# Chunk 0 of a fused Mamba-2 scan and gated feed-forward layer: two units of 64 tokens of four sequences, and one VectorE operation to join converted weights

## The chip, the core and the metric

The kernel runs on one core of a Trainium2 chip. A core has five engines with a queue each, which run side by side and wait for one another by semaphores: TensorE (PE; its weight loads are listed as PEld), VectorE (DVE), ScalarE (ACT), GpSimd (POOL) and SyncE (SP), which here only issues transfers. PE writes to PSUM, a memory of eight banks; POOL cannot read PSUM. The metric is the device time of one execution in microseconds, as the median of several runs.

## What is computed

The inputs are x (4 sequences, 8 heads, 768 tokens, 32 channels), a (4, 8, 768), B and C (4, 8, 768, 16), all float32, and two weight matrices `w_in` (256 x 2048) and `w_out` (2048 x 256), which arrive as float64. The output has 3072 rows of 256. Cut to its core:

```python
cum = np.cumsum(np.log(np.clip(a, 1e-06, 1.0)), axis=-1)       # in a chunk of tokens
L = causal * np.exp(cum[..., :, None] - cum[..., None, :])
y = ((C @ B.T) * L) @ x + (C @ state) * np.exp(cum)[..., None]
state = np.exp(cum_end) * state + (B * np.exp(cum_end - cum)).T @ x
...
h = y.reshape(B*S, H*D) @ w_in
out = (h * np.cos(h)) @ w_out
```

The result of the scan does not depend on how long the chunks are.

## The kernel before

**Chunks and steps.** The scan is done in six chunks of 128 tokens of all four sequences. Each chunk gives `yT`, 512 rows of the feed-forward layer. The layer goes through them in 16 steps a chunk: step n does `first(n)`, four matmuls of 256 columns each (L578) that give `hp` from 256 rows and 256 of the 2048 middle columns, then the gate (`k` on ACT L582, `w` on DVE L584, the cosine on ACT L589, the product `gT` on DVE L594), and, two steps later (`LAG`), `second(n)`, four matmuls (L637) that add the step's share to the output. In chunk 0, `turn_of` has step n do the rows of sequence pair u = n % 2 and middle columns of piece j = n // 2. From chunk 1 on `second` goes another way, with seven products instead of eight and sums formed on POOL (`differ`, `differ_w`).

**The weights.** They are float64 words and are converted in the kernel, in eight pieces for each matrix (256 middle columns a piece). `fetch` loads a piece. `grade` has ACT take the magnitude of the upper word (L222, `mag`) and the lower word's top bits (L220, `last`), and POOL clamp `mag` (L223). `join` has DVE shift and mask `mag` (L236), put the sign in (L238), and POOL add the two parts as integers into `w_in` or `w_out` (L246). In the loop over steps, step n grades the piece of step n+1 and joins its own: `out_j` at step 2j, `in_j` at step 2j-3. Piece `in_j` is first read by `first(2j)`, piece `out_j` by `second(2j)`.

**Chunk 0.** Sequence by sequence: `a` is spread over the partitions by matmuls against a one-hot matrix (`spread_a` L332), a scan on DVE gives the decays inside each half of 64 tokens (`decays0` L342), a matmul the decays across the halves (`cross`), PE transposes B and C (`turn`), multiplies them (`intra` L407), DVE applies the decays (L414), and PE multiplies by x (`finish` L424). Three of the four sequences are finished ahead of step 0, the fourth and the states handed to chunk 1 (`sum_up` L537, `carry` L547) in steps 0 to 2. `fill` (L101) puts matmuls without use on PE.

**Order.** The schedule is written out by hand: the order of the program is the order in every engine's queue. All loads are issued from SP, in program order: `a`, then B, C and x of three sequences, piece `in_0`, the fourth sequence, then the pieces, then the loads of chunk 1 (`rest_of_loads`). Chunks 1 and on read `a` clipped and in two forms that the kernel writes to memory itself (`a_cut`, `a_all`, L757) before it loads them again.

Of the kernel before, what the change touches and what calls it, by code (L numbers as in the profile page):

```python
# [16 lines left out]
LEAST = 2.0 ** -15  # L17
# [8 lines left out]
def kernel(  # L26
# [10 lines left out]

# [54 lines left out]
    def load(c, seqs=(0, NB), only=(B, C, x)):  # L108
# [8 lines left out]
        for dst, src in ((bc[:, 0], B), (bc[:, 1], C), (xr, x))[::2 if c > 1 else 1]:  # L117
# [3 lines left out]
            halves = c > 0 and src is not C  # L121
# [9 lines left out]

    def by_blocks(c, u):
        return c > 1

    def load_blocks(c, u):


# [33 lines left out]
    a0 = const.tile([P, P], FP32, name="a0")  # L171
    a0z = const.tile([P, P], FP32, name="a0z")
    nc.sync.dma_start(out=a0[0:NB * H], in_=a[:, :, 0:P].rearrange("b h p -> (b h) p"))
    for r in (slice(NB * H, W), slice(W, P)):
        V.memset(a0[r], 1.0)
# [31 lines left out]
    def grade(which, i, later=False, n=1):  # L207

# [6 lines left out]
        held[which, i] = list(zip(high, shares(which, mag.bitcast(U32), n), lasts))  # L217
# [3 lines left out]
        for e in range(n):  # L221
            ACT.activation(mags[e], high[e].bitcast(FP32), AF.Abs)  # L222
            G.tensor_scalar(out=mags[e], in0=mags[e], scalar1=MOST, scalar2=LEAST,  # L223
                            op0=ALU.min, op1=ALU.max)
            if not later:
                rest(e)
# [3 lines left out]
    def join(which, i):  # L230

        parts = held.pop((which, i), ())
        for e, (high, bits, last) in enumerate(parts):
            V.tensor_scalar(out=bits, in0=bits, scalar1=3, scalar2=0x3FFFFFFF,  # L236
                            op0=ALU.logical_shift_left, op1=ALU.bitwise_and)
            V.scalar_tensor_tensor(out=bits, in0=high, scalar=0xC0000000, in1=bits,  # L238
                                   op0=ALU.bitwise_and, op1=ALU.bitwise_or)
            dst = kept(which, i)  # L240
            if len(parts) > 1:
                dst = dst[:, :, e * P:(e + 1) * P]
            else:
                bits, last = (ap.rearrange("p (k f) -> p k f", k=dst.shape[1])
                              for ap in (bits, last))
            G.tensor_tensor(out=dst.bitcast(U32), in0=bits, in1=last, op=ALU.add)  # L246

    for b in range(NB):
        if b == NB - 1:
            fetch("in", 0)  # L250
        load(0, (b, b + 1))
    nc.sync.dma_start(
        out=a_in, in_=a.rearrange("(u b) h (c p) -> (b h c) u p", u=NU, p=P))
    for w in (("in", 1), ("out", 0), ("in", 2), ("out", 1), ("in", 3)):
        fetch(*w)
# [5 lines left out]
    V.memset(quarter, HALF_PI)  # L261


    unit = const.tile([P, HH * P + W], FP32, name="unit")
    G.tensor_copy(out=unit[:, 0:HH * P].rearrange("p (h i) -> p h i", h=HH),
                  in_=ident.unsqueeze(1).to_broadcast([P, HH, P]))


    ms = [scan.tile([P, 2 * H * W], FP32, tag=f"m{b}", bufs=1, name="m") for b in range(NB)]
    m_of = [t.rearrange("p (e h i) -> p e h i", e=2, h=H) for t in ms]  # L270
    m_at = [t.rearrange("p (h i) -> p h i", h=H) for t in ms]
    unit0, tos = m_of[NB - 1][:, 0], m_of[NB - 1][:, 1]
    for t in range(2):
        ts = slice(t * W, (t + 1) * W)
        V.tensor_copy(out=unit0[ts], in_=ident[ts, ts].unsqueeze(1).to_broadcast([W, H, W]))

    slot = const.tile([P, 2], FP32, name="slot")
# [7 lines left out]

    ACT.activation(const.tile([P, 1], FP32, name="sine"), quarter, AF.Sin)


    clip = dict(scalar1=1.0, scalar2=1e-6, op0=ALU.min, op1=ALU.max)
    G.tensor_scalar(out=a0z, in0=a0, **clip)  # L290
    G.memset(a0z[:, 0:P:W], 0.0)
    V.tensor_scalar(out=a0, in0=a0, **clip)


    to = const.tile([P, W], FP32, name="to")
    V.tensor_tensor_scan(out=to, data0=a0[:, W:P], data1=ones[:, 0:W], initial=1.0,
                         op0=ALU.mult, op1=ALU.mult)
    fro = const.tile([P, W], FP32, name="fro")
    V.memset(fro, 1.0)
    V.tensor_tensor_scan(out=fro[:, W - 2::-1], data0=a0[:, W - 1:0:-1],  # L300
                         data1=ones[:, 0:W - 1], initial=1.0, op0=ALU.mult, op1=ALU.mult)
    fros = const.tile([P, NB, W], FP32, name="fros")
    V.tensor_tensor(out=fros, in0=fro.unsqueeze(1).to_broadcast([P, NB, W]),
                    in1=those.unsqueeze(2).to_broadcast([P, NB, W]), op=ALU.mult)
    V.tensor_reduce(out=slot, in_=ident.rearrange("p (k t n) -> p t k n", t=2, n=N),
                    axis=mybir.AxisListType.XY, op=ALU.add)


    a0s = m_of[NB - 2]
    halves = a0z.rearrange("p (t i) -> p t i", t=2)  # L310
    for h in range(HH):
        ACT.activation(a0s[:, :, h], halves, AF.Copy, scale=mine[:, h:h + 1])
    for t in range(2):
        G.tensor_tensor(out=a0s[:, t, HH:H], in0=halves[:, t:t + 1].to_broadcast([P, HH, W]),
                        in1=mine[:, HH:H].unsqueeze(2).to_broadcast([P, HH, W]), op=ALU.mult)
    G.tensor_tensor(out=tos, in0=to.unsqueeze(1).to_broadcast([P, H, W]),
                    in1=mine.unsqueeze(2).to_broadcast([P, H, W]), op=ALU.mult)


# [4 lines left out]

    spread = {}

    def spread_a(b, tag):


        spread[b] = ps = bank([P, H, W], "a_ps", tag)  # L330
        for t in range(2):
            PE.matmul(ps[t * W:(t + 1) * W], lhsT=those[:, b:b + 1].to_broadcast([P, W]),  # L332
                      rhs=a0s[:, t], start=True, stop=True, tile_position=(0, t * W),
                      skip_group_check=True)

    def decays0(b):

        lam[0, b] = l = scan.tile([P, 2, H, W], FP32, tag="lam", bufs=4, name="lam")  # L340
        flat = "p h i -> p (h i)"
        V.tensor_tensor_scan(out=l[:, 0].rearrange(flat), data0=spread.pop(b).rearrange(flat),  # L342
                             data1=unit0.rearrange(flat), initial=0.0,
                             op0=ALU.mult, op1=ALU.add)
        G.tensor_copy(out=l[W:P, 1], in_=l[W:P, 0])
        G.memset(l[W:P, 0], 0.0)

    def cross(b, tag):

        ps = bank([P, H, W], "l_ps", tag)  # L350
        PE.matmul(ps, lhsT=fros[:, b:b + 2].rearrange("p b j -> p (b j)"), rhs=tos,
                  start=True, stop=True)
        for t in range(2):
            ACT.copy(out=lam[0, b + t][0:W, 1], in_=ps[t * W:(t + 1) * W])
            weigh(0, b + t)

    def weigh(c, b):

        scaled[c, b] = sc = scan.tile([P, H, N], FP32, tag="sc", bufs=NB, name="sc")
        l = lam[c, b][:, :, P - 1:P] if c > 0 else lam[c, b][:, 1, :, W - 1:W]  # L360
        G.tensor_tensor(out=sc, in0=raw[c][0][:, 0, heads(b)],
                        in1=l.to_broadcast([P, H, N]), op=ALU.mult)
# [23 lines left out]

    def turn(b, tag=None):

        bc = raw[0][0]
        tp = (pair("tp")[:, 0] if tag is None else bank([P, 4 * P], "tp", tag)  # L390
              ).rearrange("p (k i) -> p k i", k=4)
        for k in range(2):
            PE.transpose(tp[:, k], bc[:, k, heads(b)].rearrange("p h n -> p (h n)"), ident)

        cT = scan.tile([P, 2, P], FP32, tag="cT", name="cT")
# [340 lines left out]
    for b in range(NB):  # L736
        decays0(b)
# [177 lines left out]
```

## Time and profile before

| | |
|---|---|
| median of 3 runs | 376.96 us (376.90 to 377.03) |
| span of the profiled execution | 374.9 us |
| PE busy | 367.1 us (98%) |
| DVE busy | 286.0 us (76%) |
| POOL busy | 215.1 us (57%) |
| ACT busy | 176.0 us (47%) |
| `first(0)` starts | 17.81 us |
| `second(0)` starts | 25.71 us |
| clamp of a piece on POOL, L223, 128x512 | 0.61 to 0.93 us |
| shift and mask on DVE, L236, 128x512, mean from 25 to 72 us | 0.47 us |
| sign on DVE, L238, 128x512, mean from 25 to 72 us | 0.85 us |
| add on POOL, L246, 128x512 | 1.27 us |

The profiled execution is one run; its span goes from the first to the last instruction, and the device time of a run has about 2 us of launch and end around it. The busy share of PE is taken from modelled ends of matmuls and is no measure of how well it is used. In lines of the chain of waits the first column is the start in us, the second the time taken, then the engine and the line. In lines of the timeline the idle time before an instruction and what ended it stand in brackets. In lines of the waits the three numbers are the total in us, the count and the longest.

### The profile page before, as it was taken

The numbers are of one execution on the slowest core, as the hardware profiler recorded it, in microseconds if no ns is written. First come the engines' busy times: TensorE is split into PE (matmuls) and PEld (weight loads), VectorE is DVE, ScalarE is ACT, GpSimd is POOL, SyncE is SP. The second block draws the span as 40 slices with busy tenths as digits, with TensorE's granted clock in tenths as the row PEclk, the third lists the DMA queues.
The fourth block names the chain that finished last, engine by engine and source line by source line (L and its number), as shares of the span: only waits on it lengthen the run. The fifth ranks groups of instructions, "written<-read, shape, count | busy, mean of one in ns | idle before, by whom it ended". The sixth has DMA issues, their size and how long they took to land.

```text
span 374.9 us, 8382 instructions
## 1 busy us (share of the span) xinstructions
PE 367.1 (98%) x3108; PEld 325.4 (87%) x3108; DVE 286.0 (76%) x478; ACT 176.0 (47%) x304; POOL 215.1 (57%) x335
## 2 busy tenths in 40 slices
PE   8999999999999999999999999999999999999996
PEld 3478888889899899999899998999999989999995
DVE  8879999889799957987767987766887872554543
ACT  3887666544344434344334445434444443443442
POOL 6767555589946346665354693353775344444451
PEclk9999999999999999999999999999999999999999
DMA  7989896514545741663322655121020000010011
GB/s 84 263 239 285 243 219 117 128 15 99 151 92 78 131 108 16 84 153 77 76 54 21 91 141 131 25 51 17 4 41 8 11 21 2 0 30 0 2 28 29
DMA packets 124424, 31.52 MB, mean 84 GB/s; under 512 B 93568, under 2 KB 120288, under 8 KB 124384
## 3 DMA queue, kind: packets, MB, share of 16 engines
q1 hardware_dynamic: 124224, 30.86, 38.4%
q8 instruction: 24, 0.39, 0.4%
q14 instruction: 16, 0.13, 0.1%
q10 hardware_dynamic: 160, 0.13, 0.1%
HBM read 27.64 MB, written 3.34 MB: 83 GB/s over the span
## 4 chain that ended last, share of the span: by engine, by line
PE 83%; SPq 5%; POOL 4%; DMA 3%; DVE 2%; issue 1%; ACT 1%; POOLq 0%; DVEq 0%; ACTq 0%
PE hp L578 40%; PE o L675 29%; PE o L637 7%; SPq L127 4%; PE y L516 3%; PE g L474 2%; DMA words<-in_moe_w_in_dram 1%; POOL words L613 1%; PE y L509 1%; POOL gd L619 1%; DMA bc<-in_B_dram 1%; DMA blocks<-in_C_dram 1%; POOL gd L622 1%; PE o L720 1%; PE s_ps L537 0%
## 5 line engine op out<-in xcount | busy, mean ns | idle before, releaser
L578 PE MATMUL hp<-yT,w_in 128*128 128x256 f32 x768 | 183.7, 382 | 1.9 <-DVE gT L594 1.4
L578 PEld LDWEIGHTS hp<-yT,w_in 128*128 128x128 f32 x768 | 139.4, 190 | 21.6 <-issue 2.0
L619 POOL TENSOR_TENSOR gd<-gT 128x256 f32<-128x256 f32 x79 | 59.2, 750 | 100.0 <-DVE gT L594 91.2
L589 ACT ACTIVATE w<-w,quarter 128x512 f32<-128x512 f32 x96 | 69.2, 721 | 76.8 <-DVE w L584 76.7
L582 ACT ACTIVATE k<-hp 128x512 int32<-128x512 f32 x96 | 57.2, 595 | 82.3 <-PE hp L578 82.0
L584 DVE SCALAR_TENSOR_TENSOR w<-hp,k 128x512 f32<-128x512 f32 x96 | 65.4, 681 | 37.3 <-ACT k L582 37.1
L594 DVE TENSOR_TENSOR gT<-hp,w 128x512 f32<-128x512 f32 x96 | 65.2, 679 | 34.6 <-ACT w L589 24.8
L675 PE MATMUL o<-words,gd 128*128 128x128 f32 x474 | 65.9, 275 | 0.0
L675 PEld LDWEIGHTS o<-words,gd 128*128 128x128 f32 x474 | 59.3, 192 | 0.1
L378 DVE TENSOR_TENSOR_SCAN lam<-arow,unit 128x512 f32<-128x512 f32 x40 | 57.0, 1426 | 0.0
L675 PEld LDWEIGHTS o<-w_out,gT 128*128 128x128 f32 x316 | 47.5, 191 | 4.0
L622 POOL TENSOR_TENSOR gd<-gT,gd 128x128 f32<-128x128 f32 x79 | 45.5, 577 | 6.2
L675 PE MATMUL o<-w_out,gT 128*128 128x128 f32 x316 | 48.0, 274 | 0.0
L621 POOL TENSOR_TENSOR gd<-gT,gd 128x128 f32<-128x128 f32 x79 | 44.2, 560 | 6.2
L495 DVE TENSOR_TENSOR m<-g,lam 128x256 f32<-128x256 f32 x80 | 30.9, 415 | 0.5
L637 PE MATMUL o<-w_out,gT 128*128 128x256 f32 x128 | 30.3, 380 | 0.4 <-POOL w_out L246 0.4
L675 PE MATMUL o<-w_out,gd 128*128 128x128 f32 x158 | 30.6, 275 | 0.0
L675 PE MATMUL o<-words,gT 128*128 128x128 f32 x158 | 30.6, 275 | 0.0
L637 PEld LDWEIGHTS o<-w_out,gT 128*128 128x128 f32 x128 | 24.2, 190 | 4.0 <-POOL w_out L246 0.8
L675 PEld LDWEIGHTS o<-words,gT 128*128 128x128 f32 x158 | 24.0, 192 | 0.0
L675 PEld LDWEIGHTS o<-w_out,gd 128*128 128x128 f32 x158 | 24.0, 192 | 0.0
L692 DVE TENSOR_TENSOR sum<-ps,sum 128x256 f32<-128x256 f32 (+1 forms) x27 | 16.7, 644 | 0.6
(98 smaller groups left out, 274.5 us busy)
## 6 DMA issues: line engine op xcount, KB each, us to landing
arow<-a_cut SPq DMA_DIRECT2D x20, 512.0 KB
words<-in_moe_w_in_dram SPq DMA_DIRECT2D x8, 512.0 KB
words<-in_moe_w_out_dram SPq DMA_DIRECT2D x8, 512.0 KB
out_dram<-sum SPq DMA_DIRECT2D x18, 128.0 KB
blocks<-in_B_dram SPq DMA_DIRECT2D x128, 8.0 KB
blocks<-in_C_dram SPq DMA_DIRECT2D x128, 8.0 KB
xr<-in_x_dram SPq DMA_DIRECT2D x14, 128.0 KB
along<-a_all SPq DMA_DIRECT2D x20, 64.0 KB
```

The lines of the kernel that those rows point to most:

```text
L378: V.tensor_tensor_scan(out=lam[c, b][:, hs].rearrange("p h i -> p (h i)"), data0=rows_.rearrange("p h i -> p (h i)"), data1=unit[:, b % 2 ...
L495: V.tensor_tensor(out=m_[js, :, :, is_], in0=g_[js, :, :, is_], in1=l_[js, :, :, is_], op=ALU.mult)
L578: PE.matmul(to_[:, e], lhsT=w_in[:, k, fs], rhs=y[:, k, u], start=(k == 0), stop=(k == KT - 1), skip_group_check=True)
L582: ACT.activation(k, hp[n], AF.Copy, bias=0.25, scale=INV_2PI)
L584: V.scalar_tensor_tensor(out=w, in0=hp[n], scalar=INV_2PI, in1=k, op0=ALU.mult, op1=ALU.subtract)
L589: ACT.activation(cos, cos, AF.Sin, bias=quarter, scale=TWO_PI)
L594: V.tensor_tensor(out=gT[n], in0=hp.pop(n), in1=cos, op=ALU.mult)
L619: G.tensor_tensor(out=d[:, 0:2], in0=g[:, 1:2].to_broadcast([P, 2, P]), in1=g[:, 3::-3], op=ALU.subtract)
L621: G.tensor_tensor(out=d[:, 2], in0=g[:, 0], in1=d[:, 0], op=ALU.subtract)
L622: G.tensor_tensor(out=d[:, 3], in0=g[:, 2], in1=d[:, 2], op=ALU.subtract)
L637: PE.matmul(o[c, u][:, t], lhsT=g[:, 2 * e + t], rhs=w_out[:, 2 * j + e], start=(j == e == t == 0), stop=(j == NJ - 1 and e == 1), skip_gr ...
L675: PE.matmul(at[q], lhsT=a_[q], rhs=w[q], start=(j == 0 and q in starts), stop=(j == NJ - 1), skip_group_check=True)
```

## The change

Chunk 0 is no longer done sequence by sequence. Unit k (k = 0, 1) is tokens 64k to 64k+63 of all four sequences; two sequences lie side by side on the partitions (s), two along the free dimension (p). Unit 0 is done ahead of step 0, unit 1 in steps 0 and 1, and unit 1 takes the state that unit 0 leaves. Steps 0 and 1 do the rows of unit 0, steps 2 and 3 those of unit 1, and from step 4 on the two alternate. The loads are in another order, the loads of C for unit 0 are issued from ACT's queue, and the writes of `a_cut` and `a_all` move behind step 1's `first`. In the conversion DVE has one operation a piece, a shift combined with the sign; the sign is made by a new operation on POOL, L228 of the changed kernel. The pieces are joined at other steps. Its core (the scan's operations of a unit are like those of a sequence before, with 64 columns):

```diff
         for e in range(n):
-            ACT.activation(mags[e], high[e].bitcast(FP32), AF.Abs)
-            G.tensor_scalar(out=mags[e], in0=mags[e], scalar1=MOST, scalar2=LEAST,
-                            op0=ALU.min, op1=ALU.max)
+            ACT.activation(mags[e], high[e].bitcast(FP32), AF.Abs, scale=2.0 ** 16)
+            G.tensor_scalar(out=high[e], in0=high[e].bitcast(FP32), scalar1=0.0,
+                            scalar2=2.0 ** 31, op0=ALU.is_lt, op1=ALU.mult)
+            G.tensor_scalar(out=mags[e], in0=mags[e], scalar1=MOST * 2.0 ** 16,
+                            scalar2=LEAST * 2.0 ** 16, op0=ALU.min, op1=ALU.max)
...
-            V.tensor_scalar(out=bits, in0=bits, scalar1=3, scalar2=0x3FFFFFFF,
-                            op0=ALU.logical_shift_left, op1=ALU.bitwise_and)
-            V.scalar_tensor_tensor(out=bits, in0=high, scalar=0xC0000000, in1=bits,
-                                   op0=ALU.bitwise_and, op1=ALU.bitwise_or)
+            V.scalar_tensor_tensor(out=bits, in0=bits, scalar=3, in1=sign,
+                                   op0=ALU.logical_shift_left, op1=ALU.bitwise_or)
...
-    for b in range(NB):
-        if b == NB - 1:
-            fetch("in", 0)
-        load(0, (b, b + 1))
-    nc.sync.dma_start(
-        out=a_in, in_=a.rearrange("(u b) h (c p) -> (b h c) u p", u=NU, p=P))
-    for w in (("in", 1), ("out", 0), ("in", 2), ("out", 1), ("in", 3)):
-        fetch(*w)
+    load_bc(0, (0,))
+    load_bc(0, (1,), nc.scalar)
+    fetch("in", 0)
+    load_x(0)
+    fetch("in", 1)
+    fetch("out", 0)
+    load_bc(1)
+    load_x(1)
+    for b in range(NB):
+        nc.sync.dma_start(out=along1[:, 2 * (b % 2) + b // 2, 1:],
+                          in_=a[b, :, W:P].unsqueeze(1).to_broadcast([H, N, W]))
+    fetch("out", 1)
+    fetch("in", 2)
+    nc.sync.dma_start(
+        out=a_in, in_=a.rearrange("(u b) h (c p) -> (b h c) u p", u=NU, p=P))
+    fetch("out", 2)
+    fetch("in", 3)
...
+    fill(bank([P, 4, P], "warm", "o"), 1)
+    fill(bank([P, 2, P], "warm", "o"), 1)
+    for p in range(2):
+        spread_a(0, p)
+    decays0(0, 0)
+    turn0(0, [bank([P, 2, P], "tp", "o") for _ in range(2)])
+    decays0(0, 1)
+    spread_a(1, 0)
+    grade("in", 0, n=2)
+    inner(0)
+    fill(bank([P, 4, P], "warm", "o"), 1)
+    spread_a(1, 1)
+    for q in range(2):
+        weights(0, q)
+    join("in", 0)
+    decays0(1, 0)
+    G.tensor_copy(out=mask, in_=slot.unsqueeze(1).unsqueeze(3).to_broadcast([P, 2, 2, D]))
+    finish0(0)
+    fill(bank([P, 2, P], "warm", "o"), 1)
     grade("in", 1)
     rest = grade("out", 0, later=True)
     join("in", 1)
...
-    piece = {n: ("in", (n + 3) // 2) if n % 2 else ("out", n // 2) for n in range(NF)}
+    piece = {0: ("out", 0), 2: ("out", 1), 3: ("in", 2)}
+    for j in range(2, NJ):
+        piece[2 * j + 1] = ("out", j)
+        if j < NJ - 1:
+            piece[2 * j] = ("in", j + 1)
+    piece[2 * NJ - 2] = piece.pop(2 * NJ - 1)
...
-        return (f % 2, f // 2) if c == 0 else divmod(f, NJ)
+        if c > 0:
+            return divmod(f, NJ)
+        return divmod(f, 2) if f < 4 else (f % 2, f // 2)
...
     for n in range(NC * NF + LAG):
         c, f = divmod(n, NF)
+        if n == 2:
+            second(0)
+            finish0(1)
...
             first(n)
             if n == 0:
-                first_scan()
+                turn0(1, [bank([P, 4, P], "tp", "o")])
+                ahead()
+            if n == 1:
+                inner(1)
+                clips()
+                rest_of_loads()
...
             gated(n)
-            if n < 2:
+            if n < 2 and n in piece:
                 join(*piece[n])
+            if n == 0:
+                decays0(1, 1)
+                reach0(1)
+            if n == 1:
+                for q in range(2):
+                    weights(1, q)
...
-        if n >= LAG:
+        if n > LAG:
             second(n - LAG)
```

`turn0`, `inner`, `weights` and `finish0` are the unit's transposes, scores, decays applied to them, and products with x together with the state it leaves; `ahead` clips and fills what the scan `reach0` reads, which carries unit 0's state into unit 1; `clips` holds what was written out ahead of step 0 (the copies into `unit`, the clips, and the writes of `a_cut` and `a_all`):

```python
def weights(k, q):
    m_of[k] = units[k]
    m, l = (ap[:, :, HH * q:HH * (q + 1)].rearrange("p s (k t) i -> p k s (t i)", k=2)
            for ap in (units[k], lams[k]))
    V.tensor_tensor(out=m, in0=gs[k][q][:, :, 0:2 * P].rearrange("p k (s i) -> p k s i", s=2),
                    in1=l, op=ALU.mult)
```

## The prediction, made before any run of the changed kernel

> **What bounds the kernel now.** I read the busy rows of the page first, then the chain of waits up to 40 us, then one step of the first chunk in the timeline, then the waits of TensorE.
>
> ```profile
> PE   8999999999999999999999999999999999999996
> POOL 6767555589946346665354693353775344444451
> ```
> TensorE (PE) is full from the second slice to the last, GpSimd (POOL) is not: what is bought is time in which PE stands or runs ahead of need, and a delay of POOL costs only where PE waits for it.
>
> ```profile
> 12.29 5.41 DMA words<-in_moe_w_in_dram
> ...
> 17.73 0.69 ACT mag L222
> ...
> 21.18 1.28 POOL w_in L246
> ...
> 24.38 1.28 POOL w_out L246
> 25.66 0.04 issue
> 25.71 1.99 PE o L637 x8
> 27.70 1.73 PE hp L578 x8
> ```
> Up to 25.71 us the chain is the conversion of the weights (words land, ScalarE, POOL, VectorE, POOL); from there it is PE alone, 1.73 us for each `first` and each `second`. At 25.71 three `first` (steps 0 to 2) are done and no `second`.
>
> ```profile
> 30.99 1.89 PE L578 MATMUL hp<-yT,w_in 128*128 128x256 f32 x8
> 32.98 0.60 ACT L582 ACTIVATE k<-hp 128x512 int32<-128x512 f32 x1 [0.21 <-PE hp L578]
> 33.47 0.68 ACT L222 ACTIVATE mag<-words 128x512 f32<-128x512 f32 x1
> 34.24 0.87 POOL L223 TENSOR_SCALAR mag<-mag 128x512 f32<-128x512 f32 x1
> 34.67 0.98 DVE L238 SCALAR_TENSOR_TENSOR mag<-words,mag 128x512 uint32<-128x512 uint32 x1
> 35.73 1.27 POOL L246 TENSOR_TENSOR w_out<-mag,last 128x512 uint32<-128x512 uint32 x1 [0.62 <-DVE mag L238]
> 36.17 1.89 PE L637 MATMUL o<-w_out,gT 128*128 128x256 f32 x8
> ```
> This is step 4. Its `first` leaves PE at 32.72 (the next matmul starts there; call it E). The clamp L223 of the *next* piece starts at E+1.52, because ScalarE does it after k(4), and behind it POOL adds *this* step's piece, `out2`, done at 37.00, E+4.28. Its reader, second(4), starts at 39.62, E+6.90. So 2.6 us are spare.
>
> ```profile
> PE hp L578 <- DVE gT L594: 1.4, 3, 0.6
> PE y L516 <- POOL m L488: 0.5, 1, 0.5
> PE o L637 <- POOL w_out L246: 0.4, 1, 0.4
> ```
> PE waits for a converted piece once, 0.4 us.
>
> **Part 1, the order of the pieces.** In the changed kernel `out_j` (j = 2 to 6) is joined at step 2j+1, one step later than now; second(2j), its reader, stays behind first(2j+2). With E the end of first(2j+1), PE does second(2j-1) and first(2j+2), 2 x 1.73, and wants `out_j` at E+3.46. POOL's order there is: sign of the next piece, clamp of the next piece, add of `out_j`. The add cannot start sooner, since sign and clamp wait for ScalarE's mag, which stands behind k(2j+1). So: E+1.52 (from the fence), sign, clamp, add 1.27 (L246), 0.05 to PE.
>
> The sign operation (one input, 128x512, a word in two, written back in place as integers) is not in the trace. From below its row is the shortest L223, 0.61; from above the two-input L246, 1.27. It is nearest to L223; VectorE is in `w`, which reads PSUM, while it runs, so I take 0.62. The clamp runs beside the one VectorE operation of the join; L223 took 0.61 alone and 0.87 to 0.88 beside VectorE: I take 0.88. Sum E+4.34, with 0.06 for the hand-over E+4.40. **Stall 0.94 each, five times: 4.7 us**, and 0.3 more at step 5, where the 1.91 us scan L378 of step 4 is ahead of the join on VectorE. Bounds: 0.61+0.61 gives 0.6 each (3.0); 1.27+0.88 gives 1.6 (8.0).
>
> `out1` is joined at step 2 and read by second(1) behind first(3): wanted at E+1.73, there at E+4.40, **stall 2.7**. `in2` is joined at step 3: POOL is free at E+4.35, then sign, clamp and add (2.77) and hand-over give E+7.2; second(1) has ended at E+4.40+1.73 = E+6.13, so first(4) **waits 1.1**. The `in` pieces after it have E+5.2 and fit. Sum of part 1: 4.7+0.3+2.7+1.1 = 8.8 (bounds 6.5 and 13). Queued behind a stalled PE are only its own matmuls and then ScalarE's k; nothing catches the time up, as PE has no slack to the end.
>
> The Trainium skill (GPSIMD Engine Reference, 4.1 Engine selection) sends elementwise work to VectorE and calls one-input work on GpSimd roughly line rate; the rows beside it are L223 0.61 to 0.93 and L236 0.42. By the page the sign would be the cheap bound, and part 1 some 7 us.
>
> **Part 2, VectorE's side of the join.** L236 (0.42 to 0.53, 16 pieces, 6.7 us) goes. It is worth nothing on PE's path: in the step above VectorE ends at 35.65, and what the add waits for in the new order is POOL's own two operations.
>
> **Part 3, the first unit ahead.** Its start, from rows: `a` lands at 2.63 (wait of L290), clip 0.23 (L292), then POOL (0.41, L361) and VectorE (0.5 for 384 of L594's 512 at 0.68) one after the other, since L303 took 1.10 beside POOL's L316: 3.8. Spread 3.9 (now 4.77), two scans of 1.20 (L342) 5.5 to 7.9, transposes and copies (0.44, 0.36, 0.85) 7.85, scores 0.7 (L407), two masks of 0.64 (L414) 9.85; PE's own fill (0.9) and spread (1.0) until 10.4; 48 small matmuls at 0.63/16 (L537) 1.9; yT 0.6 (L524): **first(0) at 12.9 against 17.81.** `in0` is queued behind 2,048 packets of B rather than behind three sequences; joined by 12.1.
>
> Then `in1` follows, and POOL holds it: mag and last stand behind yT on ScalarE; mag 13.65; sign and clamp of `in1`, then both of `out0` (ordered ahead of the add), 0.62, 0.62, 0.62, 0.88 with gaps: 16.45; add 17.7. first(1) 17.7 to 19.45, inner(1) 0.7, POOL's along clip and three memsets 0.9 and `out0` 20.4: second(0) 20.45 to 22.2. VectorE: join, scan 1.2, reach 0.6 (260 of 512), w(1) 21.6; ScalarE's sine 22.4; gT 23.1; then the second unit's masks, which stand behind gT(1), 24.4. PE 40 small matmuls 1.6, yT twice 0.37: first(2) at **26.8**. There two `first` and one `second` are done, the same three units of 1.73 as now at 25.71: **+1.1 us**. The lead of 4.9 us is spent on the wait for `in1` and on a second unit that lies wholly on the path (now only y(3) and s_ps, 1.3 us, do). Bounds, all rows at their shortest and at their longest: 24.8 and 28.3, -0.9 to +2.6.
>
> **Part 4, the queues.** SP: the writes of a_cut and a_all move from 16.29 behind POOL's new place for the clips, some 23, and all of chunk 1's loads stand behind them. Cover: the first user is the scan at 36.17 now and step 4 (some 39) then; the loads now start at 17.86 into full queues (one x issue 3.43 us), then into empty ones, with arow issued at 28.6 against 26.36 and landing about 3 us on. Worth 0; without that cover 2 us at most. POOL's own five clip operations, 2.0 us, fall in 21.7 to 23.7, where it has no piece to add: 0. The C loads on ScalarE's queue delay its table load by 1.2 us, ahead of its first work at 6.5: 0. The VectorE copy of chunk 0's first output (0.67) goes to ScalarE, which is 47% busy: 0.
>
> **Sum.** Against the profiled span of 374.9: +1.1 +8.8 = +9.9. The median, 376.96, lies 2.1 us above the span (launch and end around it), which stay: **386.9 us**, with 382.5 to 391 from the bounds (376.96-0.9+6.5 = 382.6 and 376.96+2.6+13 = 392.6, of which the joint end is unlikely).
>
> **Rivals.**
> (a) The sign costs what the integer add does, 1.27: stalls 13, time 391. For it: it writes integers in place at a stride. Against it: L223 has one input as it has. 0.12.
> (b) The clock. PE has a gap of some 3 us between first(0) and first(1), with 0.44 of transposes in it; if its clock halves there, first(1) and the scores lose 1.7 to 2.4: 389. For it: two filling matmuls of four records took 3.78 at the start, 0.94 a record against 0.43 now. Against: the page grants full clock throughout and shows no such gap to judge by. 0.08. (The Trainium skill, TensorE: Matmul & The Clock Gate, Part 1, wants a whole idle window of about 3.4 us before the clock halves; by it this costs nothing. No row here shows it.)
> (c) Stalls at the low bound with a start at the low bound: 382 to 383.5. 0.10.
> (d) Faster: the lead of 4.9 us holds. The mechanism is one: `in1`'s add comes ahead of `out0`'s two operations in effect, first(2) is at 24 (-1.7), and the joins, one operation shorter on VectorE, come inside E+3.46: 375.3. It decides if sign and clamp together take under 0.6 us; the shortest L223 alone takes 0.61. 0.05.
> (e) No change to speak of, part of the lead kept against a few stalls: 0.02.
> The forecast, 383.5 to 390, has 0.63. A measurement of this kernel tells 0.2% (0.75 us) from no change: faster 0.05, same 0.02, slower 0.93.
>
> **What would show it.** Right: first(0) near 12.9 and first(2) near 26.8; TensorE's waits with `o` on POOL's add of `w_out` six times, 2.7 and then about 0.9, and `hp` on `w_in` once for 1.1; POOL's sign near 0.62. Part 3 is wrong if first(2) starts outside 24.8 to 28.3. The whole is wrong if second(4), (6) and (8) start 3.46 us behind the end of first(5), (7) and (9).

## The result, and the profile after

The changed kernel takes **408.5 us** (median of 4 runs, 408.12 to 409.82) against 377.0 for the kernel before on the same chip (376.9 to 380.52): ratio 1.0832, interval 1.0782 to 1.0883. The forecast was 386.9, its range 382.5 to 391: the side was right, the time far outside.

The page of the changed kernel: span, busy time by engine, then PE, POOL and the granted clock in 40 slices of the span.

```profile
span 407.0 us, 8692 instructions
...
PE 376.0 (92%) x3266; PEld 331.0 (81%) x3266; DVE 277.4 (68%) x454; ACT 172.2 (42%) x290; POOL 248.0 (61%) x349
...
PE   8575977777999999999999999999999999999996
...
POOL 4996697868579574466643577535368344355551
PEclk9769889899899999999999999999999999999999
```

The span grew from 374.9 to 407.0. The loss lies in the first eleven slices, where PE now stands about a quarter of the time; behind them it is full as before. POOL has 248.0 us of work instead of 215.1. PE itself is busy 8.9 us longer (376.0 against 367.1), and the row of its granted clock, 9 throughout in the kernel before, falls to 7 and 6 in the second and third slice and dips in later ones. The waits of PE (total, how often, the longest):

```profile
PE o L695 <- POOL w_out L251: 16.2, 6, 4.0
PE hp L635 <- POOL w_in L251: 5.3, 3, 3.9
PE hp L635 <- DVE lam L345: 1.9, 1, 1.9
```

There are six waits for `w_out`, 16.2 us in all; the kernel before had one, of 0.4 us. The first of the six, in the timeline (start, duration, what, idle time before and its releaser):

```profile
35.11 0.67 ACT L227 ACTIVATE mag<-words 128x512 f32<-128x512 f32 x1
...
35.87 2.53 POOL L228 TENSOR_SCALAR words<-words 128x512 uint32<-128x512 f32 x1 [2.34 <-ACT mag L227]
...
38.45 0.61 POOL L230 TENSOR_SCALAR mag<-mag 128x512 f32<-128x512 f32 x1
...
39.03 1.27 POOL L251 TENSOR_TENSOR w_out<-mag,last 128x512 uint32<-128x512 uint32 x1
...
40.35 0.93 PEld L695 LDWEIGHTS o<-w_out,gT 128*128 128x128 f32 x3 [4.44 <-POOL w_out L251]
```

This is the order that the prediction wrote down: sign and clamp of the *next* piece, then the add of `out1`, then PE. Only the sign, L228, takes 2.53 us. Over its 17 operations (15 whole pieces and two halves of `in0`) it takes this (busy total, mean ns):

```profile
L228 POOL TENSOR_SCALAR words<-words 128x512 uint32<-128x512 f32 (+1 forms) x17 | 37.4, 2200 | 13.8 <-ACT mag L227 11.6 <-issue 1.3
```

The chain that ended last shows the same in a later step, where before there was PE alone (start, duration, what):

```profile
84.78 0.56 ACT mag L227
...
85.42 2.28 POOL words L228
...
87.77 0.61 POOL mag L230
88.38 1.24 POOL w_out L251
...
89.67 1.99 PE o L695 x8
```

Where the 32.1 us of span went can be added up. first(2) starts at 32.25, where the kernel before stands at 25.71 with the same work done: 6.5. From there on PE waits 16.2 for `w_out` and 1.4 for `w_in`: 17.6. And it is busy 351.9 us from there against 343.5 with the same 2,922 records: 8.3, of which some 6.7 are four stretches of 3.4 us at half clock (13.5 us of work that takes half of that at full clock). Together 32.4, within 0.3 of the span.

### The profile page after: what moved, and what is told of

It is laid out like the page before. It is cut to its first block, busy times and chain, and to the rows that moved or that the text cites. A ratio compares the mean times of both kernels' runs of the same rounds, so it can differ in the third digit from the quotient of the medians.

```text
span 407.0 us, 8692 instructions
## 1 busy us (share of the span) xinstructions
PE 376.0 (92%) x3266; PEld 331.0 (81%) x3266; DVE 277.4 (68%) x454; ACT 172.2 (42%) x290; POOL 248.0 (61%) x349
## 4 chain that ended last, share of the span: by engine, by line
PE 74%; SPq 8%; POOL 5%; issue 4%; DVE 3%; DMA 3%; ACT 2%; DVEq 0%; ACTq 0%; POOLq 0%
PE hp L635 36%; PE o L733 28%; PE o L695 3%; SPq L110 3%; PE y L572 2%; POOL words L228 2%; PE g L530 2%; SPq L125 1%; PE y L565 1%; POOL w_out L251 1%; POOL mag L230 1%; DMA arow<-a_cut 1%; SPq L203 1%; SPq L134 1%; SPq L151 1%
## 5 line engine op out<-in xcount | busy, mean ns | idle before, releaser
L635 PE MATMUL hp<-yT,w_in 128*128 128x256 f32 x768 | 186.1, 386 | 9.1 <-POOL w_in L251 5.3
L635 PEld LDWEIGHTS hp<-yT,w_in 128*128 128x128 f32 x768 | 141.1, 192 | 30.1 <-POOL w_in L251 6.6
L676 POOL TENSOR_TENSOR gd<-gT 128x256 f32<-128x256 f32 x79 | 58.3, 738 | 101.1 <-DVE gT L651 98.3
L480 DVE TENSOR_TENSOR_SCAN lam<-arow,unit 128x512 f32<-128x512 f32 x40 | 53.6, 1341 | 0.0
L695 PE MATMUL o<-w_out,gT 128*128 128x256 f32 x128 | 36.2, 433 | 16.2 <-POOL w_out L251 16.2
L733 PEld LDWEIGHTS o<-w_out,gT 128*128 128x128 f32 x316 | 47.5, 191 | 4.0
L228 POOL TENSOR_SCALAR words<-words 128x512 uint32<-128x512 f32 (+1 forms) x17 | 37.4, 2200 | 13.8 <-ACT mag L227 11.6
L695 PEld LDWEIGHTS o<-w_out,gT 128*128 128x128 f32 x128 | 26.8, 215 | 22.9 <-POOL w_out L251 18.7
```

The lines of the kernel that those rows point to most:

```text
L228: G.tensor_scalar(out=high[e], in0=high[e].bitcast(FP32), scalar1=0.0, scalar2=2.0 ** 31, op0=ALU.is_lt, op1=ALU.mult)
L480: V.tensor_tensor_scan(out=lam[c, b][:, hs].rearrange("p h i -> p (h i)"), data0=rows_.rearrange("p h i -> p (h i)"), data1=unit[:, b % 2 ...
L635: PE.matmul(to_[:, e], lhsT=w_in[:, k, fs], rhs=y[:, k], start=(k == 0), stop=(k == KT - 1), skip_group_check=True)
L676: G.tensor_tensor(out=d[:, 0:2], in0=g[:, 1:2].to_broadcast([P, 2, P]), in1=g[:, 3::-3], op=ALU.subtract)
L695: PE.matmul(o[c, u][:, t], lhsT=g[:, 2 * e + t], rhs=w_out[:, 2 * j + e], start=(j == e == t == 0), stop=(j == NJ - 1 and e == 1), skip_gr ...
L733: PE.matmul(at[q], lhsT=a_[q], rhs=w[q], start=(j == 0 and q in starts), stop=(j == NJ - 1), skip_group_check=True)
```

## The experiments

All times are medians, each set beside the kernel before on the same chip (377.0 to 377.6 us in the median); ratios with 95% intervals stand in the table at the end of this section.

### The two halves of the change apart

`a_oldconv`: the changed kernel with the conversion of before. `b_newconv`: the kernel before with the new conversion and nothing else. The edit is the same, one way and the other:

```diff
-            ACT.activation(mags[e], high[e].bitcast(FP32), AF.Abs)
-            G.tensor_scalar(out=mags[e], in0=mags[e], scalar1=MOST, scalar2=LEAST, op0=ALU.min, op1=ALU.max)
+            ACT.activation(mags[e], high[e].bitcast(FP32), AF.Abs, scale=2.0 ** 16)
+            G.tensor_scalar(out=high[e], in0=high[e].bitcast(FP32), scalar1=0.0,
+                            scalar2=2.0 ** 31, op0=ALU.is_lt, op1=ALU.mult)
+            G.tensor_scalar(out=mags[e], in0=mags[e], scalar1=MOST * 2.0 ** 16, ...)
...
-            V.tensor_scalar(out=bits, in0=bits, ...)
-            V.scalar_tensor_tensor(out=bits, in0=high, scalar=0xC0000000, in1=bits, ...)
+            V.scalar_tensor_tensor(out=bits, in0=bits, scalar=3, in1=sign, ...)
```

> The changed kernel with the conversion of before (two VectorE operations, no sign operation on POOL). Theory 1 (the sign operation, 2.0 to 2.5 us in place of the 0.62 supposed, is nearly all of the loss): 374 to 380 us. Theory 2 (the pieces joined one step later and the second unit on PE's path cost several us even with a cheap conversion): first(2) near 26 to 27 us, PE waiting for w_out six times (2.5 us and then about 0.85 each), 384 to 388 us. Theory 3 (the halved clock of PE is a cause of its own, brought on by the gaps of the start): the clock still halves at about 16 us for 10 us.

> The kernel before with the new conversion alone; scan and pieces as before. Theory 1: POOL needs 2.2+0.61+1.27 = 4.1 us a piece where a step has 3.46, so PE waits some 0.65 us a step over 13 steps, and the start gains four sign operations of 1 to 2 us each: 390 to 400 us. Theory 2: the old schedule has 2.6 us to spare a piece, so 377 to 380 us.

Measured 388.64 and 392.85 us; the second is where the first theory had it. Each half alone costs: the start and the order of pieces 11 us, the new conversion 15 us in a kernel whose start and order are those of before. Waits of PE in `a_oldconv`:

```profile
PE o L696 <- POOL w_out L252: 7.0, 6, 2.4
PE hp L636 <- DVE gT L652: 3.7, 2, 3.1
```

The six waits for `w_out` stay without the sign, so the order makes them and the sign more than doubles them (7.0 to 16.2). The first is 2.39 us and the others 0.92 on the average, close to what the second theory expected; its time was missed by 0.6 us, and first(2) came at 28.54 instead of 26 to 27. The clock halved once, for 3.4 us from 20.2 on, not for 10 us from 16 on. The second line is a wait that the prediction lacked: first(1) stands 3.1 us for gT(0).

### The joins a step earlier

`a_oldconv_ahead`: as `a_oldconv`, with the join of a step's piece ahead of the step's own matmuls on every queue.

```diff
+            if n in piece and n > 1:
+                join(*piece[n])
             first(n)
...
-            if n in piece and n > 1:
-                join(*piece[n])
```

> The changed kernel with the conversion of before, and each join put ahead of first(n) of its step rather than behind the grading of the next piece. Theory 2: the joins then end about 3 us sooner, PE's waits for w_out go, and the time falls by 6 to 8 us against the one before it in this list, to 376 to 380 us. Theory 1: the place of the join is worth nothing, within 1 us of it.

Measured 383.89 us; the waits for `w_out` fell from 7.0 to 1.0. The time fell by 4.75 us, more than the first theory allowed and less than the 6 to 8 of the second. What is left over the kernel before, 5.7 us of span (380.6 against 374.9), adds up: first(2) at 28.67 instead of 25.71 is 3.0, one wait for `in2` 1.9, the `w_out` waits 1.0.

### What makes the sign dear

`c_forms` and `c_forms2` put extra one-input operations of no use on 128x512 words at the end of POOL's work in the kernel before, where nothing else runs; their totals say nothing, the durations are the result. `c_forms` has the pairs (is_lt, mult) and (max, min), each with and without stride and with and without integers as output; `c_forms2` varies the pair of operations.

> The kernel before with sixteen operations added on POOL behind its last work, on tiles of no use: eight forms of a 128x512 tensor_scalar, each twice. Compare and multiply (is_lt, mult) or clamp (max, min); float or integer output; a word in two or contiguous. If the compare is dear: the four is_lt forms 2 us, the four clamps 0.6. If the stride is dear: the four strided forms 2 us, the contiguous ones 0.6. If the integer output is dear: the four with integer output 2 us, the others 0.6. PE is idle there, so the time has no meaning beside that of before.

> The kernel before with twelve operations added on POOL behind its last work: 128x512 tensor_scalar with the pairs (min, max), the same to every second word as integers, (max, min), (mult, add), (mult, mult), (is_lt, mult), each twice. If the pair (min, max), which the kernel's clamps use, is the one that POOL does fast: 0.61 us for the first, 1.9 us for the pairs in another order. If the place in the program is what counts (operations one behind the other at the end are slow): all near 1.9 us, the first too.

All eight forms of `c_forms` took 1.91 to 2.01 us, so neither the stride nor the integers nor the comparison is the price: (max, min) is as dear. `c_forms2`, in the order (min, max), (min, max) with stride and integers, (max, min), (mult, add), (mult, mult), (is_lt, mult):

```profile
370.95 0.61 POOL L892 TENSOR_SCALAR fc<-fc 128x512 f32<-128x512 f32 x1
371.52 0.69 POOL L893 TENSOR_SCALAR fs<-fs 128x512 uint32<-128x512 f32 x1
372.17 2.10 POOL L894 TENSOR_SCALAR fc<-fc 128x512 f32<-128x512 f32 x1
374.35 0.62 POOL L895 TENSOR_SCALAR fc<-fc 128x512 f32<-128x512 f32 x1
375.05 0.62 POOL L896 TENSOR_SCALAR fc<-fc 128x512 f32<-128x512 f32 x1
375.76 1.94 POOL L897 TENSOR_SCALAR fc<-fc 128x512 f32<-128x512 f32 x1
```

The same engine, shape and number of inputs take 0.61 or 1.94 us, by the pair and even by its order. The clamp of before, from which the prediction priced the sign, is a pair of the quick kind.

### The sign at other prices

`l_cheap_sign`: the changed kernel with the clamp's pair on the sign's operands, so the weights lose their signs.

```diff
-                            scalar1=0.0, scalar2=2.0 ** 31, op0=ALU.is_lt, op1=ALU.mult)
+                            scalar1=2.0, scalar2=0.0, op0=ALU.min, op1=ALU.max)
```

> The changed kernel whose sign operation on POOL is a clamp (min, max) of the same operands at the same place; the weights lose their signs, everything else is done. If the sign's price is the one term of the prediction's sum that was wrong: 0.62 to 0.88 us an operation and 384 to 390 us in all, first(2) near 26.8, six waits for w_out of 2.7 and then about 0.9. If other terms were wrong as well: outside of that. If the clamp with an integer output to every second word costs the 2 us too (so that neither compare nor operand tells): 405 to 410.

391.0 us: 17.5 of the 31.5 us lost are the difference between a dear and a quick pair. It missed its interval by 1 us, and other terms were wrong as well: in the profiled execution the quick pair took 1.11 us in the median, not 0.62 to 0.88, the waits for `w_out` are still 8.5 us, and first(2) starts at 31.26 instead of near 26.8.

`b_fastsign` and `a_fastsign_ahead` make the right sign from two quick pairs, in the kernel before with the new conversion, and in the changed kernel with early joins:

```diff
-            G.tensor_scalar(out=high[e], in0=high[e].bitcast(FP32), scalar1=0.0,
-                            scalar2=2.0 ** 31, op0=ALU.is_lt, op1=ALU.mult)
+            G.tensor_scalar(out=high[e].bitcast(FP32), in0=high[e].bitcast(FP32),
+                            scalar1=-2.0 ** 50, scalar2=2.0 ** 50, op0=ALU.mult, op1=ALU.mult)
+            G.tensor_scalar(out=high[e], in0=high[e].bitcast(FP32), scalar1=2.0 ** 31,
+                            scalar2=0.0, op0=ALU.min, op1=ALU.max)
```

> The kernel before, with the new conversion, but the sign made by two operations of POOL (multiply by -2^50 twice; least with 2^31, then greatest with 0, to uint32) in place of the one compare-and-multiply. Each of the two should take 0.61 to 0.69 us as in the runs of the operation pairs (the compare pair 1.91 to 2.0 there, 2.3 to 2.5 beside VectorE), so the sign costs 1.3 us a piece and POOL has 1.3+0.61+1.27 = 3.2 us of work in a step of 3.46. THEORY (the price of the compare pair is what the new conversion costs; what it takes off VectorE, 0.43 us a piece, is worth nothing): 377 to 381 us, the waits of PE for w_out and w_in together under 3 us instead of 12.7. RIVAL 1 (one more POOL operation ahead of the clamp is enough to make every join late, whatever its price): 385 us or more. RIVAL 2 (VectorE's saving is worth something once POOL keeps up): under 376.5 us.

> The changed kernel with the sign by the same two operations of POOL and with the join of each piece put ahead of the step's own matrix work, as in the run with the old conversion that took 383.89 us. THEORY (two causes, price of the sign and joins a step late, with a dearer start of some 3 us behind them): 383 to 387 us, that is nearly all of the 31.5 us that the change lost except the start. RIVAL (a third cause lies in the new conversion or in the order of pieces): 390 us or more, with waits of PE for w_out over 5 us.

387.94 and 392.11 us: both theories missed, by 7 and by 5 us, and both times lie where a rival put them (the second rival also wanted over 5 us of waits for `w_out`; they were 4.8, with 5.6 for `w_in`). One piece on POOL in `b_fastsign`:

```profile
34.49 1.00 POOL L222 TENSOR_SCALAR words<-words 128x512 f32<-128x512 f32 x1
...
35.58 0.67 POOL L224 TENSOR_SCALAR words<-words 128x512 uint32<-128x512 f32 x1
...
36.32 0.61 POOL L226 TENSOR_SCALAR mag<-mag 128x512 f32<-128x512 f32 x1
...
36.90 1.27 POOL L247 TENSOR_TENSOR w_out<-mag,last 128x512 uint32<-128x512 uint32 x1
```

Beside the other engines the two quick pairs take 1.67 here, where the nearest forms of `c_forms2` take 1.31 alone (0.62 and 0.69). A piece takes 3.55 and small gaps: its adds follow each other every 3.7 us (25.71, 29.43, 33.14, 36.90, 40.63), a step has 3.46. In `b_newconv` they follow every 4.33 us. POOL sets the pace of the steps in both.

That left two readings: POOL's time, or one operation more in the chain ahead of the join. `b_actsign`, `a_actsign` and `a_actsign_ahead` keep the new conversion and its longer chain, but an operation of the sign's size goes to ScalarE; these weights have no signs.

```diff
-            G.tensor_scalar(out=high[e], ..., op0=ALU.is_lt, op1=ALU.mult)
+            ACT.activation(high[e], high[e].bitcast(FP32), AF.Copy, scale=0.0)
```

> The kernel before with the new conversion, but the sign operation is ScalarE's (a copy of the same 128x512 words to uint32 with scale 0, so the weights lose their signs), not POOL's; one operation of some 0.67 us more on ScalarE, which is busy 47%. POOL is left with 0.61+1.27 = 1.88 us a piece, as in the kernel before. THEORY (POOL's time a piece against the step of 3.46 us is what costs): 375.5 to 379 us, waits of PE for w_out and w_in together under 2.5 us. RIVAL 1 (the longer chain ahead of the join is enough, on whatever engine): 383 us or more, w_out waits of 5 us or more. RIVAL 2 (one VectorE operation a piece less is worth something): under 375.5 us.

> The changed kernel with the sign operation on ScalarE instead of POOL (weights without signs), all else as changed. THEORY (joins a step late and the start are what is left): 386 to 390 us, near the 388.64 of the changed kernel with the old conversion, since POOL has the same work in both. RIVAL 1 (the chain is too long): over 392 us. RIVAL 2 (VectorE's saving is worth something in this kernel): under 386 us.

> The same with the joins put ahead of the step's matrix work, as in the run of 383.89 us with the old conversion. THEORY: 382 to 386 us, w_out waits of PE under 2 us. RIVAL (VectorE's queue stands waiting for the longer chain, and so its gates come late): 389 us or more, as in the run of 392.11 us, with VectorE idle over 8 us ahead of its join operation.

377.03, 387.45 and 383.2 us, each where the theory had it. The page of `b_actsign`, and its only wait for a weight:

```profile
PE 366.8 (98%) x3108; PEld 325.5 (87%) x3108; DVE 276.6 (74%) x461; ACT 185.8 (50%) x321; POOL 216.1 (58%) x335
```

```profile
PE hp L576 <- POOL w_in L244: 0.5, 1, 0.5
```

VectorE has 9.4 us less to do than before (286.0) and the time is the same, 1.0006 (0.9982 to 1.0031). What the new conversion was to save is worth nothing in this kernel. What it cost is POOL's time: an operation of 0.67 us on ScalarE, at the same place in the chain, costs nothing. A longer operation there was not tried.

### The start

`g_scan_early` takes unit 1's second scan ahead of step 0, which frees the bank that first(1) waits for; `h_fill` leaves the wait and fills it with three matmuls of no use. Both start from `a_oldconv_ahead`.

```diff
     join("in", 1)
+    decays0(1, 1)
...
-                decays0(1, 1)
```

```diff
                 turn0(1, [bank([P, 4, P], "tp", "o")])
+                fill(bank([P, 4, P], "warm", "o"), 3)
```

> a_oldconv_ahead with the fourth scan of chunk 0 (second unit, second pair) put ahead of step 0. Theory: first(1) waits 3.1 us for gT(0) because the one free bank for hp is the one that first(0) uses, the other holding the spread a that this scan has still to read. With the scan early first(1) starts when in1 is joined, at 17.7 to 18.3 instead of 19.5, and the time falls by 1 to 2 us to 381.5 to 383. Rival: first(1) waits for something else as long, the time stays within 0.7 us.

> a_oldconv_ahead with three matmuls without use (512 columns, 0.85 us each) on PE behind the transposes of the second unit, in the gap ahead of first(1). Theory 3 (the clock halves because PE stands for about 3 us there): the clock stays full, first(1) takes 1.99 us for 2.63 and the scores 0.7 for 1.16, and the time falls by 1 to 1.5 us. Rival: the gap is not what halves the clock; it halves all the same and the time stays within 0.7 us or grows by the fills.

384.96 and 385.24 us: no gain over 383.89, where each was expected to take 1 to 2 us less. In `h_fill` first(1) ran at full clock in 1.97, as its theory had it, and the clock halved later instead. In `g_scan_early` first(1) comes at 17.69 as expected, and the waits turn up elsewhere: second(0) now stands 2.2 us for `out0`, whose add is on POOL behind the clip of the row decays, and the clock halves later and longer. Its first(2) and first(3):

```profile
29.49 6.04 PE L636 MATMUL hp<-yT,w_in 128*128 128x256 f32 x16 [0.46 <-ACT yT L441]
```

Sixteen matmuls in 6.04 us that take 3.72 at full clock. In `h_fill` the same two took 6.69 us.

`best`, `best2` and `best3` take out one after the other the waits that each trace showed, and put filling matmuls behind second(0) (four in `best`, one in the others): in `best`, `out0` is joined ahead of gT(0) and of the clip, `in2` is prepared earlier, unit 1's weights stand ahead of gT(1); in `best2`, the product of the reaches is ahead of POOL's clips, and from step 3 the pieces have the order of before; in `best3`, `out1` is joined ahead of unit 1's scores. The core of it:

```diff
             if n == 1:
                 inner(1)
+                reach0(1)
                 clips()
...
+            if n == 0:
+                join(*piece[n])
+                ahead()
             gated(n)
...
-    piece = {0: ("out", 0), 2: ("out", 1), 3: ("in", 2)}
...
+    piece = {n: ("in", (n + 3) // 2) if n % 2 else ("out", n // 2) for n in range(NF) if n != 1}
```

> The changed start with the old conversion, and the waits of the start that the runs showed taken out together: the second scan of unit 1 ahead of step 0, out0 joined ahead of gT(0) and ahead of the clip of the row decays, in2 prepared a step earlier, the scan of the reaches and the weights of unit 1 ahead of gT(1), four filling matmuls behind second(0) so that TensorE's clock has no gap of over 1.5 us. THEORY (the loss that was left, 5.7 us, was waits and the halved clock, not work): first(2) at 26.5 to 27.5 us and 377 to 380 us, clock full in all slices. RIVAL 1 (the start of the change is bound by VectorE's work before unit 1's weights, whatever the order): first(2) at 28 us or later, 382 us or more. RIVAL 2 (the start is now ahead of the one before): first(2) before 25.7, under 376.5 us.

> The run before it (381.92 us) with three things of its own trace mended: the product of the reaches (POOL, L377) stood behind the clips of the decays and behind clamps that waited for words, and came at 25.87 us where its scan ended at 22.17; the order of pieces after step 3 is that of the kernel before (each one step earlier); out1's low word and in2 are prepared behind unit 1's scores. One filling matmul in place of four. THEORY (of the 4.8 us that were left, 3.2 are the start's and 1.8 the joins a step late, and both are order, not work): scores of unit 1 from about 23 us, first(2) at 25 to 26 (25.71 is where the kernel before stands at the same amount of work), no wait for w_out over 0.5 us, 375 to 378 us. RIVAL 1 (DMA or VectorE bounds the start whatever the order): first(2) at 27 us or later, 379 us or more. RIVAL 2 (the start in two units is worth its price when nothing waits): under 375 us.

> The run of 381.61 us with out1 joined ahead of unit 1's scores and in2 prepared behind first(2), so that no work of ScalarE on pieces stands between yT and first(2). THEORY (order, not work): first(2) at 26 to 27.5 us with full clock, 376.5 to 379 us. RIVAL 1 (a wait takes its place again, or the clock halves): 380.5 us or more. RIVAL 2 (the start pays): under 375.5 us.

381.92, 381.61 and 382.25 us: none beats the kernel before, and all three theories missed. Each mended wait came back under another name. In `best2` unit 1's products with x are done by 26.6, but first(2) starts at 29.26 and runs into half clock; in `best3` it stands for nothing that the profile shows:

```profile
29.39 3.72 PE L636 MATMUL hp<-yT,w_in 128*128 128x256 f32 x16 [2.95 <-issue]
```

yT had been ready from 27.1. In `h_fill` PE stood 1.6 us in the same way, at 27.8, between two matmuls of one group. What PE waited for there is not settled, and so it stays open whether the start in two units could be made level. A further wait of the start, for the load of unit 1's C, is in several of these profiles but not in that of the changed kernel: 2.5 us in `l_cheap_sign`, 2.3 in `a_actsign_ahead`, 1.4 in `best2`, 0.8 in `best3`. In `best3` the clock was full and first(2) still 3.7 us behind 25.71; without that one wait it would be 0.7 us behind.

### All together

| conversion | order and start of before | changed | changed, joins ahead |
|---|---|---|---|
| of before | 377.0 | 388.64, 1.0283 (1.0227 to 1.0339) | 383.89, 1.0166 (1.0101 to 1.0232) |
| new | 392.85, 1.0392 (1.0345 to 1.044) | 408.5, 1.0832 (1.0782 to 1.0883) | not tried |
| new, sign as one quick pair | not tried | 391.0, 1.0355 (1.0329 to 1.0382) | not tried |
| new, sign as two quick pairs | 387.94, 1.0254 (1.0194 to 1.0315) | not tried | 392.11, 1.0347 (1.0275 to 1.0419) |
| new, operation on ScalarE | 377.03, 1.0006 (0.9982 to 1.0031) | 387.45, 1.0278 (1.025 to 1.0307) | 383.2, 1.0155 (1.0121 to 1.019) |

The ratios of the first row and of the last agree in every column within their intervals. So of the 31.5 us lost, 21 are the sign on POOL (408.5 less 387.45), 4.3 the joins a step late (387.45 less 383.2), and some 6 the start with its own waits. The sign costs more in the changed kernel (21) than in the one before (15.8): some 6.7 us of the 21 are the four later stretches at half clock, which follow its longer waits and which the profile of `a_actsign` does not have. Starts that were mended by hand gave 381.6, ratio 1.0105 (1.0064 to 1.0146), with the conversion of before.

## Why the prediction was right on the side and wrong on the time

**The step that failed is the price of the sign in part 1.** The prediction said of it: "from below its row is the shortest L223, 0.61; from above the two-input L246, 1.27 ... I take 0.62". It takes 2.2 us on the average, 2.37 in the stretch of the stalls (32 to 110 us). The upper bound was no bound: one input is not cheaper than two when the pair of operations is one that POOL does slowly, and the only row of its kind in the trace, the clamp, happens to be a quick pair. The rest of part 1 holds. With 2.37 in place of 0.62 and the clamp at its 0.61, its own sum for the add is E+5.88, each of the five stalls 2.42, `out1` 4.15 and `in2` 2.6 late, together some 19 us. Measured are 17.6: 16.2 in six waits for `w_out`, the number and the places that it named (4.04 for `out1`, 2.33 to 2.69 in the five that are alike), and 1.4 in two for `w_in` of 0.7 each, where it had one. A quick pair at that place would not have cost 0.62 either: in `l_cheap_sign` it took 1.11. And PE had waited for a converted piece twice in the kernel before, not once: 0.3 us for `w_in` at first(0) besides the 0.4 for `w_out`.

**Part 2 was right:** VectorE's operation is worth nothing. `b_actsign` shows it to 0.3%, with 9.4 us less work on VectorE.

**Part 3 was wrong for two reasons.** The first is the banks. first(0) was put at 12.9 and came at 14.87, having stood 1.93 us for the scan L345; without that wait it would have come at 12.94. The two banks of `hp` are those into which `a` of unit 1 is spread, and a bank is free only when its scan is done. The same holds for the second bank and first(1): with the quicker conversion it stands 3.1 us until gT(0) (`a_oldconv`), which the program puts ahead of that scan on VectorE; `g_scan_early`, with the scan moved, had first(1) at 17.69, the 17.7 of the prediction. The second is the sign again. In the changed kernel itself that wait lies under a longer one: `in1`'s add stood behind two signs on POOL (1.99 and 2.49 us) and first(1) started at 21.96. first(2) came at 32.25, 4 us past the upper bound.

**Rival (b), the clock, came true as well,** though it was given 0.08 and one gap: PE ran at half clock in five stretches, one of some 10 us and four of 3.4. It was busy 19.9 us in them, with work that takes half of that at full clock: 3.2 us are lost in the long one and 6.7 in the four. The first of them, in windows of the changed kernel (PE busy, its instructions, granted clock, DMA share, GB/s):

```profile
15.00:20.00 5.00, 3.11 (x12) 0.63 0.63 129
20.00:25.00 5.00, 3.04 (x7) 0.50 0.99 367
25.00:30.00 5.00, 4.16 (x55) 0.85 0.27 67
```

first(1), in the second of them, took 3.78 us instead of 1.99. **Rival (a)** had the right term and too small a price: it stopped at 1.27 and 391. It was the range's upper end too, since 13 was the most that part 1 could then cost. Rivals (c), (d) and (e) needed a cheaper sign than there was.

**Part 4** (queues) held: no wait of PE for a load of chunk 1 is in the changed kernel's list, though the loads came later, and VectorE stood ahead of none of its first six scans over `arow`.

## What to carry to other kernels

An operation that the trace lacks is priced by a row of the same engine *and the same operations*, not of the same shape and number of inputs; where there is none, the upper bound is a multiple (here 2.37 against a bound of 1.27), and a kernel that runs the form alone for a microsecond settles it. An engine that is busy 57% over the whole can still set the pace of one stage: here POOL's work per piece, 1.88 us before and 4.1 to 4.3 after, was to be held against the step's 3.46. And a step that is moved ahead needs its buffers ahead too: ask of each bank who held it last.

## What the runs showed of the hardware that was not expected

On POOL a one-input operation on 128x512 words takes 0.61 to 0.69 us with (min, max), (mult, add) or (mult, mult), and 1.91 to 2.10 with (is_lt, mult) or (max, min). Stride and output type change this by 0.1 us at most; they were varied for (min, max) and the slow pairs. Beside the work of the other engines the slow pair takes up to 2.55, and a quick one up to 1.6. The Trainium skill's GPSIMD Engine Reference, 4.1 Engine selection, calls one-input work on this engine roughly line rate; the quick pairs agree with it and the slow ones do not.

PE's clock halved after gaps of 2.3 us in some cases and not in others. Two steps of the changed kernel, the same eight matmuls after nearly the same wait:

```profile
56.84 3.43 PE L695 MATMUL o<-w_out,gT 128*128 128x256 f32 x8 [2.33 <-POOL w_out L251]
68.11 1.99 PE L695 MATMUL o<-w_out,gT 128*128 128x256 f32 x8 [2.41 <-POOL w_out L251]
```

What decides, by these traces, is where the gap lies. In that of the changed kernel all ten changes of the granted clock, five down and five up, fall on a grid of 3.41 us: down at 16.28, 40.17, 57.24, 77.71 and 101.61, up at 26.51, 43.58, 60.65, 81.13 and 105.02. Cut along this grid, the stretches at full clock from 12.86 to 108 us with less than 2 us of PE's work are these:

| stretch, us | PE busy in it, us | clock in the next |
|---|---|---|
| 12.86 to 16.28 | 1.49 | 0.50 |
| 36.76 to 40.17 | 0.00 | 0.50 |
| 53.82 to 57.24 | 1.09 | 0.50 |
| 64.06 to 67.48 | 1.64 | 1.00 |
| 74.30 to 77.72 | 1.03 | 0.50 |
| 87.96 to 91.37 | 1.70 | 1.00 |
| 98.20 to 101.61 | 1.36 | 0.50 |

So two of the five waits of 2.33 to 2.69 us for `w_out` were not followed by half clock: the grid cuts them (65.70 to 68.11 and 86.98 to 89.67) into parts of at most 1.8 us. The three others leave 2.05 us or more of idle time in one stretch, and the wait of 4.04 covers a whole one. At half clock the same goes on until a stretch is full: those at 16.28 and 19.69, with 1.83 and 1.14 us of work, were followed by half clock, and those with over 3.2 us by full. The other profiles with changes have the same spacing at other offsets. The border is not sharp: after 1.51 us (`a_oldconv_ahead`) the clock stayed, after 1.78 (`h_fill`) it fell. A wait of 2.3 us can thus cost 4, by where the grid happens to lie. The Trainium skill, TensorE: Matmul & The Clock Gate, Part 1, speaks of a whole idle window of about 3.4 us before the clock falls; the length agrees with the 3.41 here, but stretches with up to 1.49 us of work in them were enough.

Executions of one kernel differ with the clock: four of `a_oldconv_ahead` took 382.39, 383.22, 384.56 and 386.82 us at mean granted clocks of 0.994, 0.991, 0.990 and 0.987. That kernels which differ in a few waits scatter by 1 to 2 us about what their waits add up to may come from this too; that is argued, not shown.
